# Outputs copied out two batch rows at a time, a re-ordered prologue and qd of chunk 1 on GpSimd, in a decay-attention and softplus-FFN kernel

## The chip, the cores and the metric

The kernel runs on one core of a Trainium2 chip. The metric is the device time of one execution in microseconds (us). Each kernel is run several times; the profile comes from one further execution on the same chip, whose own time is given beside its span (first to last instruction).

## What is computed

Decaying linear attention over 4 batch rows, 8 heads, 768 positions and head size 64, in blocks of 64 positions with a state carried from block to block, and then a feed-forward layer with softplus, 512 to 2048 to 512. All data are float32.

```python
rel = pos[:, None] - pos[None, :]
Dmask = np.where(rel >= 0, lam[:, None, None] ** rel[None, :, :], 0.0)
lam_pow = lam[:, None, None] ** (pos[None, :, None] + 1)
for b in range(nb):                                   # 12 blocks of 64
    intra = einsum('bhic,bhjc->bhij', qb, kb) * Dmask[None]
    intra = einsum('bhij,bhjd->bhid', intra, vb)
    inter = einsum('bhid,bhde->bhie', qb * lam_pow[None], kv_state)
    out[:, :, sl] = intra + inter
    kv_state = lam_block * kv_state + einsum('bhsd,bhse->bhde', kb * rev_pow, vb)
x = out.transpose(0, 2, 1, 3).reshape(B * S, H * D)
h = x @ w_in
y = (np.maximum(h, 0) + np.log1p(np.exp(-np.abs(h)))) @ w_out
```

## The kernel before

**Tiling.** The 768 positions are six chunks of 128 (two blocks of 64). A *unit* g is one chunk and one pair of heads: units 0 to 3 are chunk 0, units 4 to 7 chunk 1, 24 in all. A chunk's feed-forward layer has 16 *steps*, one per 128 hidden features; step number s runs over all chunks, 96 in all. The two large products keep float32 accuracy by splitting each operand into a high part (rounded to the float32r type) and a low part (the remainder): three matmuls take the place of one.

**A unit** has these parts. `k_decay` makes kd, k times the decay to the block's end (L259, two ScalarE instructions in every chunk). `q_decay` makes qd, q times the decay from the block's start (L265, two multiplications, on GpSimd in chunk 0 and on VectorE later). `mm_scores` (L273) multiplies k by q and kd by v into a two-bank PSUM tile. `mask_scores` (L303, VectorE) masks the scores; `first_states` (L317, ScalarE) or `second_states` and `update_states` (VectorE, L311) carry the state. `mm_out` (L287) makes the attention output; `x_high` (L333, ScalarE) and `x_low` (L340, VectorE) split it for the next product. For chunk 0 the tiles of kd, qd and masked scores are each unit's own; later they come from four rotating buffers (tag b2).

**A step** has `mlp1` (L359), 12 matmuls over the four pairs of heads; `chain_act` and `chain_lo` (L349, L355: softplus and copy on ScalarE, subtraction on VectorE); and, three steps later, `mlp2` (L373), 12 matmuls, three for each batch row, which accumulate over a chunk's 16 steps in two PSUM tiles `o` of two banks each. Tile 0 holds batch rows 0 and 1, tile 1 rows 2 and 3; the next chunk's tiles use the same banks. In a chunk's last `mlp2` each row's matmuls are followed at once by the row's copy out of PSUM, on ScalarE for even rows and on VectorE for odd ones, and by its transfer to memory on SP's queue. The last chunk cuts each row in two halves, one for each of the two engines, each with its own transfer on ScalarE's or SP's queue; its last `mlp2` takes two steps at once, six matmuls a row.

**The weights** arrive as packed blocks k = 0 to 31 in the order in which the steps use them, and are turned into high and low parts once: `w_scale` (two ScalarE instructions, L203 and L205), `w_bits` (three on VectorE, L209, L210, L213), `w_hi` (L216, a copy, on ScalarE unless VectorE is given) and `w_lo` (L220, VectorE). Blocks 0, 1 and 2 are converted one by one in the prologue, the rest in groups of two by the first steps: step s finishes one group and begins the next.

**What sets the order.** Nothing is reordered: each engine executes its instructions in the order in which the program lists them, and waits where data or buffers are not ready. The prologue is written out by hand (L420 to L464), with `begin(p)` (scores), `middle(p)` (state and mask) and `end(p)` (output) for the four units of chunk 0, the conversion of blocks 0 to 2 in between, and `keep_warm(n)`: n matmuls on zeros. The loop after it (L471) runs each step's parts in a fixed order. Scores of unit s//4 + 4 come at s % 4 = 1, its output at s % 4 = 3, and the kd of the next unit at s % 4 = 0. Loads are issued on SP, in an order of their own.

Of the kernel before, what the change touches and what calls it, by code (L numbers as in the profile page):

```python
# [7 lines left out]
F32 = mybir.dt.float32  # L8
# [6 lines left out]
B, H, S, D = 4, 8, 768, 64  # L15
C = 128
T = 64
NCH = S // C
NP = H // 2
NG = NCH * NP  # L20
# [11 lines left out]
def decay_attention_softplus_ffn(  # L32
# [7 lines left out]
    nc = tc.nc  # L40
# [7 lines left out]
    def t8(shape, dt, name):  # L48
        return sb.tile(shape, dt, tag="b8", bufs=21, name=name)
# [41 lines left out]
    def q_of(g):  # L91
        return part(g, 0, 0)
# [4 lines left out]
    def kt_of(g):  # L97
        return part(g, 1, 0)
# [46 lines left out]
    def keep_warm(n):  # L145
        for _ in range(n):
            nc.tensor.matmul(warm_ps, lhsT=warm[:, :128], rhs=warm, start=True, stop=True)  # L147

    keep_warm(30)

# [47 lines left out]
    def w_scale(ks):  # L200

        c = conv[ks[0]] = t4([128, len(ks), DM], U32, f"c{ks[0]}")
        nc.scalar.activation(c.bitcast(F32), raw_at(ks, 1).bitcast(F32), AF.Copy, scale=2.0**-112)  # L203

        nc.scalar.activation(raw_at(ks, 0), raw_at(ks, 0), AF.Copy, scale=2.0**-29)  # L205

    def w_bits(ks):
        c = conv[ks[0]]
        nc.vector.tensor_single_scalar(out=c, in_=c, scalar=3, op=ALU.logical_shift_left)  # L209
        nc.vector.scalar_tensor_tensor(  # L210
            out=c, in0=raw_at(ks, 1), scalar=0x80000000, in1=c, op0=ALU.bitwise_and, op1=ALU.bitwise_or
        )
        nc.vector.tensor_add(out=c, in0=c, in1=raw_at(ks, 0))  # L213

    def w_hi(ks, copy=nc.scalar.copy):
        copy(out=w_at(ks)[:, 0], in_=conv[ks[0]].bitcast(F32))  # L216

    def w_lo(ks):
        w = w_at(ks)
        nc.vector.tensor_sub(out=w[:, 1], in0=conv.pop(ks[0]).bitcast(F32), in1=w[:, 0])  # L220
# [19 lines left out]
    def heads(g):  # L240
        p = g % NP
        return slice(2 * p, 2 * p + 2)

    def first_chunk(g):
        return g < NP
# [6 lines left out]
    def own(g, n, name):  # L252
        if not first_chunk(g):
            return t2([128, B, 2, 64], F32, f"{name}_{g}")
        if g not in spares:
            spares[g] = t8([128, 3, B, 2, 64], F32, f"own_{g}")
        return spares[g][:, n]

    def k_decay(g):  # L259
        kd = kds[g] = own(g, 0, "kd")  # L260
        for t in range(2):
            h = heads(g).start + t
            nc.scalar.activation(kd[:, :, t], kt_of(g)[:, :, t], AF.Copy, scale=rp1[:, h : h + 1])  # L263

    def q_decay(g, eng):  # L265
        qd = qds[g] = own(g, 1, "qd")
        r = hi if first_chunk(g) else slice(0, 128)
        for t in range(2):
            w = lp[r, heads(g).start + t : heads(g).start + t + 1, :].broadcast_to([r.stop - r.start, B, T])
            eng.tensor_mul(out=qd[r, :, t], in0=q_of(g)[r, :, t], in1=w)  # L270


    def mm_scores(g, w):  # L273
# [59 lines left out]
    def x_high(g, w):  # L333

        nc.scalar.copy(  # L335
            out=x_of(g // NP, g % NP)[:, 0].rearrange("q (b s i) -> q s b i", b=B, s=2),
            in_=w[:, :, 0:256].rearrange("q s (b i) -> q s b i", b=B),
        )

    def x_low(g, w):  # L340
        x = x_of(g // NP, g % NP).rearrange("q n (b s i) -> q n s b i", b=B, s=2)
        nc.vector.tensor_sub(  # L342
            out=x[:, 1], in0=w[:, :, 0:256].rearrange("q s (b i) -> q s b i", b=B), in1=x[:, 0]
        )
# [14 lines left out]
    def mlp1(s, ps_=range(NP)):  # L359
        c, f = divmod(s, NF)  # L360
        if s not in h_tiles:
            h_tiles[s] = bank(f"h{s}")
        w = w_of(f, 0)
        for p in ps_:
            cs = slice(p * 128, (p + 1) * 128)
            x = x_of(c, p)
            for n, (i, j) in enumerate(((0, 0), (1, 0), (0, 1))):
                nc.tensor.matmul(  # L368
                    h_tiles[s], lhsT=w[:, i, cs], rhs=x[:, j, :],
                    start=p == 0 and n == 0, stop=p == NP - 1 and n == 2,  # L370
                )

    def mlp2(ss):  # L373
        c = ss[0] // NF
        ends = ss[-1] % NF == NF - 1
        if ss[0] % NF == 0:
            o_tiles[c] = [pair(f"o{c}_{bp}") for bp in range(2)]
        if ends:
            parts = [t8([128, B, 512], F32, f"ob{c}_{n}") for n in range(2 if c == NCH - 1 else 1)]
        for b in range(B):  # L380
            for s in ss:
                f = s % NF
                g, w = g_tiles[s], w_of(f, 1)
                for n, (i, j) in enumerate(((0, 0), (0, 1), (1, 0))):
                    nc.tensor.matmul(  # L385
                        o_tiles[c][b // 2][:, b % 2], lhsT=g[:, i, b * 128 : (b + 1) * 128], rhs=w[:, j],
                        start=f == 0 and n == 0, stop=f == NF - 1 and n == 2,
                    )
            if not ends:
                continue  # L390
            src = o_tiles[c][b // 2][:, b % 2]
            rows = slice(b * S + c * C, b * S + (c + 1) * C)
            if c == NCH - 1:
                nc.scalar.copy(out=parts[0][:, b, 0:256], in_=src[:, 0:256])
                nc.scalar.dma_start(out=out[rows, 0:256], in_=parts[0][:, b, 0:256])
                nc.vector.tensor_copy(out=parts[1][:, b, 0:256], in_=src[:, 256:512])
                nc.sync.dma_start(out=out[rows, 256:512], in_=parts[1][:, b, 0:256])
            else:
                if b % 2:
                    nc.vector.tensor_copy(out=parts[0][:, b], in_=src)  # L400
                else:
                    nc.scalar.copy(out=parts[0][:, b], in_=src)  # L402
                nc.sync.dma_start(out=out[rows, :], in_=parts[0][:, b])


    w0, z = {}, {}
# [1 line left out]
    def begin(p):  # L408
        w0[p] = pair(f"xy{p}")
        mm_scores(p, w0[p])  # L410

    def middle(p):
        first_states(p, w0[p])
        mask_scores(p, w0[p])

    def end(p):
        z[p] = work(f"z{p}")
        mm_out(p, z[p])

    for p in range(NP):  # L420
        q_decay(p, nc.gpsimd)
    k_decay(0)
    begin(0)
    keep_warm(2)
# [1 line left out]
    k_decay(1)  # L426
    end(0)
    x_high(0, z[0])
    x_low(0, z[0])
    begin(1)  # L430
    keep_warm(3)
    middle(1)
    end(1)
    x_high(1, z[1])
    x_low(1, z[1])
    k_decay(2)
    keep_warm(5)
    begin(2)
    keep_warm(5)
    w_scale([0])  # L440
    middle(2)
    k_decay(3)
    w_bits([0])
    end(2)
    x_high(2, z[2])
    x_low(2, z[2])
    begin(3)
    keep_warm(3)
    middle(3)
    w_hi([0], nc.vector.tensor_copy)  # L450
    w_lo([0])
    w_scale([1])
    end(3)
    mlp1(0, range(NP - 1))
    x_high(3, z[3])
    x_low(3, z[3])
    mlp1(0, range(NP - 1, NP))
    w_bits([1])
    w_hi([1], nc.vector.tensor_copy)
    w_lo([1])  # L460
    w_scale([2])
    k_decay(NP)
    w_bits([2])
    w_hi([2])  # L464

# [5 lines left out]
    for s in range(last + LAG):  # L471

        scores, outs = None, None
        if s % 4 == 1 and s // 4 + NP < NG:
            scores = s // 4 + NP
        if s % 4 == 3 and s // 4 + NP < NG:
            outs = s // 4 + NP
        if 0 <= s - 1 < last:
            chain_act(s - 1)
            chain_lo(s - 1)  # L480
        old, new = (w_group(s + 1) if s else [2]), w_group(s + 2)
        if s and old:
            w_hi(old)
        if new:
            w_scale(new)
        if old:
            w_lo(old)
        if new:
            w_bits(new)
        if s == last + LAG - 2:  # L490
            mlp2([s - LAG, s - LAG + 1])
        elif 0 <= s - LAG < last - 1:
            mlp2([s - LAG])
        if scores is not None:
            w = work(f"w{scores}")
            mm_scores(scores, w)
            mask_scores(scores, w)
            if scores < 2 * NP:
                second_states(scores - NP)
            update_states(scores, w)  # L500
            q_decay(scores, nc.vector)
        if s % 4 == 0 and s and s // 4 + NP < NG:
            k_decay(s // 4 + NP)
        if outs is not None:
            w = work(f"z{outs}")
            mm_out(outs, w)
            x_high(outs, w)
            x_low(outs, w)
        if 0 < s < last:
            mlp1(s)  # L510
        w_load(2 * s + (9 if s < 9 else 7))
        if s % 4 == 3:
            load_upto(s // 4 + NP + 2)
# [40 lines left out]
```

## Time and profile before

| | |
|---|---|
| median of 3 runs | 642.11 us (640.03, 642.11 and one of 2590.12) |
| the profiled execution | 640.66 us, span 638.9 us, mean granted TensorE clock 0.992 |
| PE busy | 609.5 us, 95% of the span, 5296 matmuls |
| VectorE (DVE) busy | 231.2 us, 36% |
| ScalarE (ACT) busy | 209.6 us, 33% |
| GpSimd (POOL) busy | 7.0 us, 1% |
| bytes moved | 48.99 MB, mean 77 GB/s |

The page gives shares of the whole span. The 40 slices below them are read next, since they tell stages apart: each slice is a fortieth of the span, and each digit the busy tenths of an engine in it. The chain of work that ended last goes back from the last instruction to what released it, and so on; a row is start, duration, engine, what it writes and the line. In the views of groups, idle time of an engine is listed with what ended it. "issue" is time in which the profile shows nothing that an engine waits for. Each float32 matmul of the attention appears as two instructions; a matmul's end is modelled.

### The profile page before, as it was taken

The numbers are of one execution on the slowest core, as the hardware profiler recorded it, in microseconds if no ns is written. First come the engines' busy times: TensorE is split into PE (matmuls) and PEld (weight loads), VectorE is DVE, ScalarE is ACT, GpSimd is POOL, SyncE is SP. The second block draws the span as 40 slices with busy tenths as digits, with TensorE's granted clock in tenths as the row PEclk, the third lists the DMA queues.
The fourth block names the chain that finished last, engine by engine and source line by source line (L and its number), as shares of the span: only waits on it lengthen the run. The fifth ranks groups of instructions, "written<-read, shape, count | busy, mean of one in ns | idle before, by whom it ended". The sixth has DMA issues, their size and how long they took to land.

```text
span 638.9 us, 11805 instructions
## 1 busy us (share of the span) xinstructions
PE 609.5 (95%) x5296; PEld 491.4 (77%) x5296; DVE 231.2 (36%) x360; ACT 209.6 (33%) x335; POOL 7.0 (1%) x16
## 2 busy tenths in 40 slices
PE   8787999998999998999998999999899999899996
PEld 6566778786888886888886888888688888688884
DVE  4389999953313313133133133132221221111111
ACT  2466776832222222322313222222323222222221
POOL 3000000000000000000000000000000000000000
PEclk9888999999999999999999999999999999999999
DMA  8993112323200221300111500102500100100001
GB/s 302 407 379 133 67 68 92 140 67 112 88 1 2 68 67 66 133 1 1 67 37 47 183 1 2 67 1 67 178 21 1 43 25 2 66 1 0 2 1 66
DMA packets 15747, 48.99 MB, mean 77 GB/s; under 512 B 1873, under 2 KB 2897, under 8 KB 15697
## 3 DMA queue, kind: packets, MB, share of 16 engines
q1 hardware_dynamic: 15120, 47.72, 20.8%
q8 instruction: 41, 0.67, 0.4%
q10 hardware_dynamic: 576, 0.52, 0.3%
q14 instruction: 10, 0.07, 0.0%
HBM read 41.95 MB, written 6.29 MB: 76 GB/s over the span
## 4 chain that ended last, share of the span: by engine, by line
PE 82%; DVE 10%; ACT 5%; issue 2%; DVEq 0%; ACTq 0%
PE h L368 37%; PE o L385 36%; DVE c L213 3%; PE w L280 2%; DVE c L210 2%; PE warm_ps L147 2%; PE z L294 2%; PE z L298 2%; DVE st L311 1%; DVE c L209 1%; DVE w L220 1%; ACT ob L402 1%; DVE g L357 1%; ACT c L203 1%; ACT l L351 1%
## 5 line engine op out<-in xcount | busy, mean ns | idle before, releaser
L385 PE MATMUL o<-w,g 128*128 128x512 f32 x1152 | 280.2, 390 | 11.7 <-ACT ob L402 9.1
L368 PE MATMUL h<-x,w 128*128 128x512 f32 x1152 | 285.1, 397 | 0.9 <-ACT l L351 0.9
L385 PEld LDWEIGHTS o<-w,g 128*128 128x128 f32 x1152 | 215.2, 188 | 61.4 <-ACT ob L402 13.3
L368 PEld LDWEIGHTS h<-x,w 128*128 128x128 f32 x1152 | 214.6, 189 | 47.9 <-ACT l L351 1.4
L357 DVE TENSOR_TENSOR g<-l,g 128x512 fp32r<-128x512 f32 x96 | 66.3, 691 | 285.5 <-ACT g L353 285.5
L351 ACT ACTIVATE l<-h 128x512 f32<-128x512 f32 x96 | 57.3, 597 | 306.4 <-PE h L368 298.2
L353 ACT CAST g<-l 128x512 fp32r<-128x512 f32 x96 | 59.6, 621 | 3.1
L342 DVE TENSOR_TENSOR x<-z,x 128x512 fp32r<-128x512 f32 x24 | 16.6, 690 | 48.5 <-ACT x L335 48.5
L311 DVE SCALAR_TENSOR_TENSOR st<-st,lam_c,w 64x256 f32<-64x256 f32 x72 | 31.7, 480 | 0.9
L335 ACT CAST x<-z 128x512 fp32r<-128x512 f32 x24 | 14.0, 584 | 50.7 <-PE z L298 50.7
L280 PEld LDWEIGHTS w<-att 64*64 64x64 f32 x640 | 21.2, 135 | 7.3 <-issue 5.6
L294 PEld LDWEIGHTS z<-qd,st 64*64 64x64 f32 x640 | 17.5, 136 | 11.6 <-issue 11.5
L282 PE MATMUL w<-att,kd 64*64 64x64 f32 x576 | 23.8, 222 | 2.6 <-ACT kd L263 2.4
L294 PE MATMUL z<-qd,st 64*64 64x64 f32 x640 | 21.5, 226 | 4.4 <-DVE qd L270 4.4
L280 PE MATMUL w<-att 64*64 64x64 f32 x640 | 24.7, 222 | 0.0
L306 DVE TENSOR_TENSOR a<-w,mask 128x512 f32<-128x512 f32 x20 | 13.8, 691 | 29.8 <-PE w L282 22.4
L216 ACT CAST w<-c 128x1024 fp32r<-128x1024 f32 (+1 forms) x16 | 16.0, 998 | 25.6 <-DVE c L213 25.6
L282 PEld LDWEIGHTS w<-att,kd 64*64 64x64 f32 x576 | 20.6, 135 | 3.4 <-ACT kd L263 3.4
L263 ACT ACTIVATE kd<-att,rp 128x256 f32<-128x256 f32 x40 | 18.1, 501 | 12.5 <-DMA att<-in_att 12.5
L220 DVE TENSOR_TENSOR w<-c,w 128x1024 fp32r<-128x1024 f32 (+1 forms) x18 | 19.9, 1106 | 4.6 <-ACT w L216 4.4
L213 DVE CUSTOM_DVE_ANT_0 c<-raw,c 128x2048 uint16<-128x2048 uint16 (+1 forms) x18 | 19.9, 1108 | 2.7 <-DVE c L210 0.6
L298 PE MATMUL z<-a,att 64*64 64x64 f32 x640 | 20.5, 221 | 0.0
(42 smaller groups left out, 205.2 us busy)
## 6 DMA issues: line engine op xcount, KB each, us to landing
att<-in_att SPq DMA_DIRECT2D x48, 512.0 KB, 4.7
raw<-in_wts SPq DMA_DIRECT2D x32, 512.0 KB, 10.2
out_dram<-ob SPq DMA_DIRECT2D x20, 256.0 KB, 2.3
out_dram<-ob ACTq DMA_DIRECT2D x4, 128.0 KB, 1.7
out_dram<-ob SPq DMA_DIRECT2D x4, 128.0 KB, 1.7
lam_b<-in_lam SPq DMA_DIRECT2D x1, 4.0 KB, 2.8
```

The costliest lines, as they stand in the source:

```text
L213: nc.vector.tensor_add(out=c, in0=c, in1=raw_at(ks, 0))
L220: nc.vector.tensor_sub(out=w[:, 1], in0=conv.pop(ks[0]).bitcast(F32), in1=w[:, 0])
L280: nc.tensor.matmul(w[r, 0, cols], lhsT=k[r, b, t], rhs=q[r, b, t], start=True, stop=True)
L282: nc.tensor.matmul(w[half(1 - s), 1, cols], lhsT=kd[r, b, t], rhs=v[r, b, t], start=True, stop=True)
L294: nc.tensor.matmul(w[half(t), s, cols], lhsT=st[r, b, t], rhs=qd[r, b, t], start=True, stop=False)
L298: nc.tensor.matmul(w[half(t), s, cols], lhsT=v[r, b, t], rhs=a[r, b, t], start=s == 0 and first_chunk(g), stop=True,)
L311: nc.vector.scalar_tensor_tensor(out=to[:, :, t], in0=of[:, :, t], scalar=lam_c[r, h : h + 1], in1=u[:, :, t], op0=ALU.mult, op1=ALU.add,)
L351: nc.scalar.activation(l_tiles[s], h_tiles.pop(s), AF.Softplus)
L353: nc.scalar.copy(out=g_tiles[s][:, 0, :], in_=l_tiles[s])
L357: nc.vector.tensor_sub(out=g[:, 1, :], in0=l_tiles.pop(s), in1=g[:, 0, :])
L368: nc.tensor.matmul(h_tiles[s], lhsT=w[:, i, cs], rhs=x[:, j, :], start=p == 0 and n == 0, stop=p == NP - 1 and n == 2,)
L385: nc.tensor.matmul(o_tiles[c][b // 2][:, b % 2], lhsT=g[:, i, b * 128 : (b + 1) * 128], rhs=w[:, j], start=f == 0 and n == 0, stop=f == NF ...
```

## The change

It has five parts.

1. *Outputs.* In a chunk's last `mlp2`, copies and transfers come after every second batch row: the even row's copy on ScalarE and the odd row's on VectorE, each of a whole row of 512. In the last chunk the rows are no longer cut in halves; ScalarE's queue issues the even rows' transfers and SP's the odd ones'.
2. *kd of chunk 0* is one VectorE multiplication by a broadcast operand, in place of two ScalarE instructions.
3. *qd* is one instruction a unit in place of two. Units 0 to 7 have it on GpSimd, before only units 0 to 3; from unit 8 on it stays on VectorE. It is issued with kd, at s % 4 = 0 in place of s % 4 = 1.
4. *The order of the prologue.* The conversion of block 0 lies between units 0 to 2 and that of block 1 around units 2 and 3; the copies `w_hi` of blocks 0 and 1 are ScalarE's; the parts of `mlp1(0)` run as soon as their units are done; 18 of 48 warm-up matmuls go.
5. *kd of unit 4* moves from the end of the prologue into step 0, behind the scaling of blocks 3 and 4.

```diff
-    keep_warm(30)
+    keep_warm(26)
...
     def k_decay(g):
         kd = kds[g] = own(g, 0, "kd")
+        if first_chunk(g):
+            w = rp1[:, heads(g)].rearrange("q (o t w) -> q o t w", o=1, w=1).broadcast_to([128, B, 2, D])
+            nc.vector.tensor_mul(out=kd, in0=kt_of(g), in1=w)
+            return
...
-    def q_decay(g, eng):
+    def q_decay(g):
         qd = qds[g] = own(g, 1, "qd")
         r = hi if first_chunk(g) else slice(0, 128)
-        for t in range(2):
-            w = lp[r, heads(g).start + t : heads(g).start + t + 1, :].broadcast_to([r.stop - r.start, B, T])
-            eng.tensor_mul(out=qd[r, :, t], in0=q_of(g)[r, :, t], in1=w)
+        eng = nc.gpsimd if g < 2 * NP else nc.vector
+        w = lp[r, heads(g), :].rearrange("q (o t) i -> q o (t i)", o=1).broadcast_to([r.stop - r.start, B, 2 * T])
+        eng.tensor_mul(
+            out=qd[r].rearrange("q b t i -> q b (t i)"), in0=q_of(g)[r].rearrange("q b t i -> q b (t i)"), in1=w
+        )
...
         if ends:
-            parts = [t8([128, B, 512], F32, f"ob{c}_{n}") for n in range(2 if c == NCH - 1 else 1)]
+            ob = t8([128, B, 512], F32, f"ob{c}")
...
-            if not ends:
+            if not ends or b % 2 == 0:
                 continue
-            src = o_tiles[c][b // 2][:, b % 2]
-            rows = slice(b * S + c * C, b * S + (c + 1) * C)
-            if c == NCH - 1:
-                nc.scalar.copy(out=parts[0][:, b, 0:256], in_=src[:, 0:256])
-                nc.scalar.dma_start(out=out[rows, 0:256], in_=parts[0][:, b, 0:256])
-                nc.vector.tensor_copy(out=parts[1][:, b, 0:256], in_=src[:, 256:512])
-                nc.sync.dma_start(out=out[rows, 256:512], in_=parts[1][:, b, 0:256])
-            else:
...
+            for n, copy in ((b - 1, nc.scalar.copy), (b, nc.vector.tensor_copy)):
+                copy(out=ob[:, n], in_=o_tiles[c][n // 2][:, n % 2])
+                queue = nc.scalar if c == NCH - 1 and n % 2 == 0 else nc.sync
+                queue.dma_start(out=out[n * S + c * C : n * S + (c + 1) * C, :], in_=ob[:, n])
...
     x_high(0, z[0])
+    begin(1)
+    keep_warm(2)
     x_low(0, z[0])
-    begin(1)
-    keep_warm(3)
     middle(1)
+    w_scale([0])
     end(1)
+    w_bits([0])
+    k_decay(2)
     x_high(1, z[1])
     x_low(1, z[1])
-    k_decay(2)
-    keep_warm(5)
+    w_hi([0])
     begin(2)
-    keep_warm(5)
-    w_scale([0])
     middle(2)
+    w_lo([0])
     k_decay(3)
-    w_bits([0])
     end(2)
+    mlp1(0, range(2))
     x_high(2, z[2])
+    begin(3)
     x_low(2, z[2])
-    begin(3)
-    keep_warm(3)
     middle(3)
-    w_hi([0], nc.vector.tensor_copy)
-    w_lo([0])
     w_scale([1])
+    w_bits([1])
+    mlp1(0, range(2, 3))
     end(3)
-    mlp1(0, range(NP - 1))
     x_high(3, z[3])
     x_low(3, z[3])
-    mlp1(0, range(NP - 1, NP))
-    w_bits([1])
-    w_hi([1], nc.vector.tensor_copy)
+    mlp1(0, range(3, 4))
+    w_hi([1])
+    w_scale([2])
     w_lo([1])
-    w_scale([2])
-    k_decay(NP)
     w_bits([2])
     w_hi([2])
...
             update_states(scores, w)
-            q_decay(scores, nc.vector)
-        if s % 4 == 0 and s and s // 4 + NP < NG:
+        if s % 4 == 0 and s // 4 + NP < NG:
             k_decay(s // 4 + NP)
+            q_decay(s // 4 + NP)
```

More of the change, by code (lines that the diff above doesn't have):

```diff
@@ L388, in mlp2 @@
                     )
-            if not ends:
+            if not ends or b % 2 == 0:
                 continue
-            src = o_tiles[c][b // 2][:, b % 2]
-            rows = slice(b * S + c * C, b * S + (c + 1) * C)
-            if c == NCH - 1:
-                nc.scalar.copy(out=parts[0][:, b, 0:256], in_=src[:, 0:256])
-                nc.scalar.dma_start(out=out[rows, 0:256], in_=parts[0][:, b, 0:256])
-                nc.vector.tensor_copy(out=parts[1][:, b, 0:256], in_=src[:, 256:512])
-                nc.sync.dma_start(out=out[rows, 256:512], in_=parts[1][:, b, 0:256])
-            else:
[L399 to L403, printed above, removed]
+            for n, copy in ((b - 1, nc.scalar.copy), (b, nc.vector.tensor_copy)):
+                copy(out=ob[:, n], in_=o_tiles[c][n // 2][:, n % 2])
+                queue = nc.scalar if c == NCH - 1 and n % 2 == 0 else nc.sync
+                queue.dma_start(out=out[n * S + c * C : n * S + (c + 1) * C, :], in_=ob[:, n])
     w0, z = {}, {}
@@ L420, in decay_attention_softplus_ffn @@
     for p in range(NP):
-        q_decay(p, nc.gpsimd)
+        q_decay(p)
     k_decay(0)
```

## The prediction

> **What bounds the kernel now.** I read the page's slices first, then the chain of work that ended last, then the groups and the timelines of single stages.
>
> ```profile
> PE   8787999998999998999998999999899999899996
> DVE  4389999953313313133133133132221221111111
> PEclk9888999999999999999999999999999999999999
> L385 PE MATMUL o<-w,g 128*128 128x512 f32 x1152 | 280.2, 390 | 11.7 <-ACT ob L402 9.1
> ```
>
> A slice is 16 us. There are three stages. Up to about 37 us is the prologue, with a clock below full. From there to about 119 us the DVE digits stand at 9: the conversion of the weights on VectorE sets the pace. After that only PE is full. Its one visible wait there is in the last row: the second MLP product waits for ACT's copy of an output, 9.1 us in all.
>
> That wait costs more than its row says. First the chain over two ordinary double steps and one in which a chunk of outputs ends, then that end:
>
> ```profile
> 132.25 2.95 PE h L368 x12
> ...
> 144.45 2.96 PE h L368 x12
> ...
> 159.05 2.95 PE h L368 x12
> ...
> 171.25 2.95 PE h L368 x12
> ```
> ```profile
> 148.68 0.49 ACT ob L402
> ...
> 149.22 1.67 PE o L385 x6
> ...
> 150.91 0.59 ACT ob L402
> ...
> 151.55 0.96 PE o L385 x3
> ```
>
> From 132.25 to 144.45 and from 159.05 to 171.25 the same pair of steps takes 12.20 us; from 144.45 to 159.05 it takes 14.60. The difference, 2.40, is the price of one chunk end. PE wants to write batch row 1 into the other half of the two-bank PSUM tile from which ACT copies row 0, and waits until that copy is over; the same happens between rows 2 and 3. Part of the 2.40 is the matmul pipeline, which runs empty each time.
>
> **The outputs in pairs.** Row 1's matmuls now come before row 0's copy, and row 3's before row 2's. The tile that PE writes next is the other pair, so nothing reads it. Five chunk ends times 2.40 is 12.0 us. What hides the copies then is the following first MLP product, 12 matmuls or 2.72 us at 0.227 each (worked out below), against copies that need these times:
>
> ```profile
> L400 DVE COPY ob<-o 128x512 f32<-128x512 f32 x10 | 6.9, 692 | 12.6 <-PE o L385 12.6
> L402 ACT COPY ob<-o 128x512 f32<-128x512 f32 x10 | 5.8, 582 | 8.7 <-PE o L385 8.7
> DVE own L306 <- ACT st L319: 8.4, 4, 5.0
> ```
>
> The third row (the view of waits) matters for their order: there too ACT and DVE read the two halves of one PSUM tile, and DVE begins only when ACT is done. So a pair takes 0.58 + 0.69 and two gaps of 0.03, about 1.33 us, one after the other. The last pair is free 1.33 us after its matmuls; PE asks for it no sooner than after 12 matmuls of the other product. Without that cover each chunk end would cost 1.33. Behind the copies on ACT stands the next softplus, which waits for that product anyway.
>
> The last chunk has no cover, and its copies were halves before:
>
> ```profile
> 624.64 4.09 PE o L385 x18
> ...
> 629.64 3.03 PE o L385 x12
> ...
> 633.58 1.67 PE o L385 x6
> ...
> 635.27 0.38 ACT ob L394
> ...
> 635.67 0.42 DVE ob L396
> ```
> ```profile
> out_dram<-ob SPq DMA_DIRECT2D x20, 256.0 KB, 2.3
> out_dram<-ob SPq DMA_DIRECT2D x4, 128.0 KB, 1.7
> ```
>
> The 18 matmuls that end at 628.73 take 0.227 us each. The other 18 would end at 628.73 + 4.08 = 632.81 without the two waits, instead of 635.24: 2.43 gained. Against it: the last two copies take 1.33 instead of 0.85 (635.24 to 636.09), 0.48 lost, and the last transfer is 256 KB, 2.3 us to landing instead of 1.7, 0.6 lost. Net 1.4 us. Bounds: 0.8 (ACT's copy behind a late transfer issue) to 2.0 (copies side by side).
>
> The Trainium skill ("PSUM — Partial Sum Buffer", section on bank collisions) says that two engines on different banks do not disturb each other; the two halves are different banks. By that rule the copies could run side by side, and the end would come some 0.6 us sooner; the wait row above speaks for the order that I take, since it is the program that makes DVE wait.
>
> **The prologue.** Its end is what the DVE stage starts from.
>
> ```profile
> 1.45 8.64 PE warm_ps L147 x30
> ...
> 16.35 1.68 issue
> ...
> 19.35 2.43 PE warm_ps L147 x5
> 22.92 1.36 PE warm_ps L147 x5
> 28.45 1.96 issue
> ```
> ```profile
> 16.35:28.45 12.10, 10.15 (x254) 7.79 (x254) 5.17 (x9) 6.21 (x12) 0.68 (x1) 0.86 1.03 407
> ```
> ```profile
> 42.30 1.05 ACT L216 CAST w<-c 128x1024 fp32r<-128x1024 f32 x1 [1.21 <-DVE c L213]
> ```
> ```profile
> 7.95 0.91 ACT L263 ACTIVATE own<-att,rp 128x256 f32<-128x256 f32 x2 [5.94 <-DMA att<-in_att]
> 31.66 0.69 DVE L342 TENSOR_TENSOR x<-z,x 128x512 fp32r<-128x512 f32 x1 [2.89 <-ACT x L335]
> 32.27 0.42 DVE L209 TENSOR_SCALAR c<-c 128x512 uint32<-128x512 uint32 x1
> 34.64 0.69 DVE L220 TENSOR_TENSOR w<-c,w 128x512 fp32r<-128x512 f32 x1
> 36.53 0.69 DVE L213 CUSTOM_DVE_ANT_0 c<-raw,c 128x1024 uint16<-128x1024 uint16 x1
> ```
>
> *Order of the conversion.* From x_low of unit 3 at 31.66, VectorE is never idle: conversion of weight block 1 (32.27 to 34.64, with the copy of its high part), its low part at 34.64, block 2 until 37.22. In the change the bits of block 1 are made before that x_low, in the 2.89 us in which VectorE waits for it, and the high part is ACT's. So the work between 32.27 and 34.64 leaves this place: 2.4 us. ACT's copy (about 0.6, as the row of L402 for that size) runs beside x_low (0.69). If the cover were too short (the bits are 1.9 of the 2.4 us), the excess would come back; bounds 1.5 to 2.4.
>
> *PE's part.* Four warm-up matmuls fewer at the start is 4 x 0.227 = 0.9 us sooner, and kd of unit 0 is there: one multiplication of 0.69 us, started at 7.95, ends before the 26 are through. The 0.69 for a kd on VectorE is the row of the equally large x_low, against 0.91 for ACT's two; three of the four stand where VectorE waits, and the fourth, kd of unit 3, lies ahead of x_low of unit 2, behind PE's own work. The warm-ups after unit 1 (2.43) leave the chain. Those at 22.92 hid the state copy and the mask (0.58 and 0.69, by the rows of that size), which stay. Six matmuls of the first MLP product come in before unit 3, at 0.23 to 0.43 us each (1.4 to 2.6). And two stalls named "issue" stay: PE stops at 16.35 and again 254 matmuls and 254 weight loads later, with the DMA engines full (share 1.03). I read this as the fetch of instructions (the page has a DMA queue of that name) behind the loads. It comes at a fixed count of instructions, and 36 fewer do not carry either stall out of the prologue; a stall met earlier may simply last longer. So x_high of unit 3 comes between 0 and 2.6 us sooner than at 31.05; I take 1.5.
>
> Prologue together: 2.4 + 1.5 = 3.9 us (bounds 1.5 and 5.0). kd of unit 4, moved behind the scaling of blocks 3 and 4 on ACT, costs 0.9 us of ACT ahead of the first softplus, and ACT idles 1.21 us before its copy at 42.30: nothing, or 0.9 if that cover is gone. No DMA is issued in another place on SP; the loads run ahead of their use by more than the shift.
>
> **qd on GpSimd.** The DVE stage ends where PE waits for kd of unit 7, at 118.97:
>
> ```profile
> 51.29 0.76 DVE L270 TENSOR_TENSOR qd<-att,lp 128x256 f32<-128x256 f32 x2
> ```
> ```profile
> 118.17 0.80 ACT kd L263 x2
> ```
> ```profile
> 13.06 1.42 POOL L270 TENSOR_TENSOR own<-att,lp 64x256 f32<-64x256 f32 x2 [2.42 <-DMA att<-in_att]
> 14.32 0.69 DVE L342 TENSOR_TENSOR x<-z,x 128x512 fp32r<-128x512 f32 x1 [1.76 <-ACT x L335]
> ```
>
> Units 4, 5 and 6 have their qd before that point, 0.76 us each with VectorE busy without a break around it; 3 x 0.76 = 2.3 us. GpSimd does as many elements per partition in 1.42, and it is issued a step before the scores and read three steps after. Unit 7's lies behind the point and gains nothing, nor does merging two instructions into one from chunk 2 on: VectorE is at a third there. What GpSimd's work costs VectorE beside it no row shows directly. Nearest is the pair above: VectorE's 14.32 instruction overlaps GpSimd's and still takes 0.69. So zero; the other bound is the whole GpSimd instruction, 3 x 1.42 = 4.3 us, a net loss of 2.0.
>
> **Sum**, against the profiled execution's 640.66 (span 638.9; the median of the three runs is 1.45 higher): 640.66 - 12.0 - 1.4 - 3.9 - 2.3 = 621.1 us.
>
> **Rivals.**
> *GpSimd holds VectorE.* In the stage at 9s nearly every VectorE instruction reads two operands from SBUF; the row at 14.32 reads one from PSUM, so it excludes little. If GpSimd's instruction blocks them for its length, three of them cost 4.3 and save 2.3: 640.66 - 17.3 + 2.0 = 625.4. The Trainium skill ("SBUF — State Buffer", "Who interferes with whom") states just this: a VectorE instruction with two SBUF inputs contends with a GpSimd one that reads SBUF, and the later one waits for all of it. No row here tests that rule.
> *The prologue gives nothing.* Fewer warm-ups, a slower clock (already 0.86 between the stalls), and stalls that end when the fetch ends: 640.66 - 15.7 = 625.0. For it speaks that the second stall's end at 30.41 may hang on the loads alone; against it, that 2.4 of the 3.9 do not depend on PE.
> *The wait at the chunk end only moves*, to the next chunk's first rows: half of 12.0 remains, about 627.1. Against it: 2.7 us of cover for 1.33.
> *Slower: each copy waits for the transfer of the row before it*, since all four fill one tile. Then the four copies take 2 x 1.27 + 3 x 2.3 = 9.4 us from 148.7 on, to 158.1, and PE, 30 matmuls after 147.41 (the rest of this product, the other one, the first pair), wants the second pair at 154.2: 3.9 lost per chunk end, 19.5 in all, and 6.9 in the last. 640.66 - 12.0 + 19.5 + 6.9 - 1.4 - 6.2 = 647.5. It decides from a stall of 2.4 per chunk end on. Against it:
>
> ```profile
> 149.19 4.48 SPq L403 DMA_DIRECT2D out_dram<-ob  x4
> 150.29 0.69 DVE L400 COPY ob<-o 128x512 f32<-128x512 f32 x1 [0.88 <-PE o L385]
> ```
>
> The copy of row 1 began 1.1 us after row 0's transfer was issued, before its 2.3 were over, in the same tile.
>
> **Chances.** Forecast 0.48, GpSimd's hold 0.27, no gain in the prologue 0.15, the moved wait 0.08, slower 0.02. The range goes from 617.0 (prologue 5.0, tail 2.0, and some waits of VectorE for ACT gone too) to 627.0, which takes in three rivals' centres but not two of them together. 2% is 12.8 us, about what a measurement of this kernel tells from no change: 627.9 is the line. The chunk ends alone nearly reach it, and any one other term carries it over; faster 0.88, within 10 in 100, slower 2 in 100.
>
> **What would show it.** In the profile after: pairs of steps across a chunk end at 12.2 us; no wait of PE for an output copy; the last copies on ACT and DVE in turn; x_high of unit 3 near 29.5 and block 2's bits finished near 33.3 instead of 37.22; VectorE instructions of unchanged length with no gaps while GpSimd works (gaps of over 1 us would be the hold); PE free of the DVE stage near 112.8. A chunk end above 12.2, a stall in the prologue that outlasts 31 us, or an idle VectorE beside GpSimd each prove one term wrong.

## The result, and the profile after

| | before | after |
|---|---|---|
| median of the runs | 641.55 us (4 runs, one of them 2590.12) | 625.56 us (4 runs, 625.08 to 625.74) |
| profiled execution, span | 640.66, 638.9 us | 625.08, 623.3 us |
| VectorE, ScalarE, GpSimd busy | 231.2, 209.6, 7.0 us | 230.2, 208.2, 12.7 us |

The ratio, which leaves out the run of 2590.12 us, is 0.9757, with a 95% interval of 0.9737 to 0.9778: about 16 us faster. The forecast was 621.1 (617 to 627), so the direction and the range held, and the gain fell short by 4 us. The measured 625.1 is also what two of the rivals had named (GpSimd's hold 625.4, no gain in the prologue 625.0), so the time alone cannot tell them apart. The rows can.

The end of a chunk first: rows of the chain that ended last (start, duration, engine, what it writes, line), over the same stretch of steps as before.

```profile
118.28 2.99 PE h L374 x12
...
130.52 2.95 PE h L374 x12
...
142.72 2.95 PE h L374 x12
...
154.92 2.95 PE h L374 x12
...
167.12 2.95 PE h L374 x12
```
```profile
L391 PE MATMUL o<-w,g 128*128 128x512 f32 x1152 | 276.4, 389 | 0.0
```

Every pair of steps now takes 12.20 us, the one with the chunk end (142.72 to 154.92) too; it was 14.60. The group of the second product (from the page) has no idle time left in front of it, where it had 11.7 us. The last chunk runs through as well:

```profile
610.88 8.17 PE o L391 x36
...
619.07 0.59 ACT ob L398
...
619.69 0.69 DVE ob L398
```

36 matmuls without a break, then the last pair's copies in turn, ScalarE before VectorE, as forecast. From the last copy's end to the end of the span it is 2.92 us, against 2.81 before: the larger transfer cost 0.1, not 0.6.

Now the prologue and the conversion stage. First x_high of unit 3, with which the prologue ends, before the change, then the same in the changed kernel (ScalarE's timelines) with VectorE's rows from there on:

```profile
31.05 0.58 ACT L335 CAST x<-z 128x512 fp32r<-128x512 f32 x1 [2.93 <-PE z L298]
```

```profile
32.03 0.59 ACT L341 CAST x<-z 128x512 fp32r<-128x512 f32 x1 [0.71 <-PE z L304]
```
```profile
32.08 0.69 DVE L213 CUSTOM_DVE_ANT_0 c<-raw,c 128x1024 uint16<-128x1024 uint16 x1
32.69 0.68 DVE L348 TENSOR_TENSOR x<-z,x 128x512 fp32r<-128x512 f32 x1
33.46 0.69 DVE L220 TENSOR_TENSOR w<-c,w 128x512 fp32r<-128x512 f32 x1
...
35.35 0.69 DVE L213 CUSTOM_DVE_ANT_0 c<-raw,c 128x1024 uint16<-128x1024 uint16 x1
```

Block 1's bits do lie before x_low of unit 3 (32.69), and block 2 is done at 36.04, 4.01 us after x_high began; before, it took 6.17 us. But x_high itself came 1 us later, not 1.5 sooner. And VectorE instructions beside GpSimd's are longer. GpSimd's rows for units 5, 6 and 7 (unit 4's qd lies in the prologue, at 24.81), and VectorE's beside them:

```profile
41.52 1.30 POOL L274 TENSOR_TENSOR qd<-att,lp 128x512 f32<-128x512 f32 x1 [15.45 <-PE w L288]
...
66.56 1.51 POOL L274 TENSOR_TENSOR qd<-att,lp 128x512 f32<-128x512 f32 x1 [23.73 <-ACT g L359]
...
110.27 1.82 POOL L274 TENSOR_TENSOR qd<-att,lp 128x512 f32<-128x512 f32 x1 [42.20 <-DMA att<-in_att]
```
```profile
42.19 1.72 DVE L220 TENSOR_TENSOR w<-c,w 128x1024 fp32r<-128x1024 f32 x1 [0.51 <-ACT w L216]
...
66.83 1.78 DVE L363 TENSOR_TENSOR g<-l,g 128x512 fp32r<-128x512 f32 x1
...
111.08 2.10 DVE L213 CUSTOM_DVE_ANT_0 c<-raw,c 128x2048 uint16<-128x2048 uint16 x1
```

These three take 1.22, 0.69 and 1.23 us elsewhere. Each ends about its usual length after GpSimd's instruction has ended: 41.52 + 1.30 = 42.82, and 42.19 + 1.72 = 43.91 is 1.09 later.

### The profile page after: what moved, and what is told of

Same layout as the page of the kernel before. It is cut to its first block, busy times and chain, and to the rows that moved or that the text cites. A ratio compares the mean times of both kernels' runs of the same rounds, so it can differ in the third digit from the quotient of the medians.

```text
span 623.3 us, 11732 instructions
## 1 busy us (share of the span) xinstructions
PE 604.4 (97%) x5278; PEld 492.1 (79%) x5278; DVE 230.2 (37%) x336; ACT 208.2 (33%) x327; POOL 12.7 (2%) x16
## 4 chain that ended last, share of the span: by engine, by line
PE 84%; DVE 11%; issue 2%; ACT 2%; DVEq 0%; ACTq 0%
PE h L374 38%; PE o L391 37%; DVE c L210 2%; PE w L286 2%; DVE c L213 2%; PE z L300 2%; PE z L304 2%; DVE w L220 1%; PE warm_ps L147 1%; DVE c L209 1%; DVE st L317 1%; DVE g L363 1%; ACT w L216 1%; PE w L288 1%; PE xy L286 0%
## 5 line engine op out<-in xcount | busy, mean ns | idle before, releaser
L391 PE MATMUL o<-w,g 128*128 128x512 f32 x1152 | 276.4, 389 | 0.0
L286 PE MATMUL w<-att 64*64 64x64 f32 x640 | 26.0, 226 | 0.0
L216 ACT CAST w<-c 128x1024 fp32r<-128x1024 f32 (+1 forms) x18 | 17.2, 956 | 22.4 <-DVE c L213 22.4
L220 DVE TENSOR_TENSOR w<-c,w 128x1024 fp32r<-128x1024 f32 (+1 forms) x18 | 20.4, 1132 | 4.0 <-ACT w L216 3.8
L213 DVE CUSTOM_DVE_ANT_0 c<-raw,c 128x2048 uint16<-128x2048 uint16 (+1 forms) x18 | 20.8, 1156 | 2.5
L210 DVE SCALAR_TENSOR_TENSOR c<-raw,c 128x1024 uint32<-128x1024 uint32 (+1 forms) x18 | 19.9, 1107 | 0.6
```

Source lines behind the costliest of these rows:

```text
L210: nc.vector.scalar_tensor_tensor(out=c, in0=raw_at(ks, 1), scalar=0x80000000, in1=c, op0=ALU.bitwise_and, op1=ALU.bitwise_or)
L286: nc.tensor.matmul(w[r, 0, cols], lhsT=k[r, b, t], rhs=q[r, b, t], start=True, stop=True)
L391: nc.tensor.matmul(o_tiles[c][b // 2][:, b % 2], lhsT=g[:, i, b * 128 : (b + 1) * 128], rhs=w[:, j], start=f == 0 and n == 0, stop=f == NF ...
```

## The experiments

Three times, all read from each run's profile, separate what the runs mix: W, the end of the first warm-up matmuls in the chain; X, the start of x_high of unit 3; and F, the first step of the steady stage (the row at 120.05 before and at 118.28 after). X - W is the rest of the prologue, F - X the conversion stage.

| run | W | X | X - W | F - X | ratio to before (95%) |
|---|---|---|---|---|---|
| before | 10.09 | 31.05 | 20.96 | 89.00 | |
| after | 10.46 | 32.03 | 21.57 | 86.25 | 0.9757 (0.9737 to 0.9778) |
| e1_pairs_only | 11.35 | 32.80 | 21.45 | 88.98 | 0.9798 (0.9781 to 0.9815) |
| e2_rest_only | 10.06 | 32.48 | 22.42 | 86.24 | 0.9974 (0.9964 to 0.9984) |
| e3_qd_vector | 8.97 | 31.34 | 22.37 | 84.39 | 0.9719 (0.9706 to 0.9733) |
| e4_qd_twice | 9.49 | 32.11 | 22.62 | 88.43 | 0.9802 (0.9787 to 0.9817) |
| e5_writes_only | 9.69 | 32.46 | 22.77 | 87.53 | 0.9788 (0.9771 to 0.9804) |
| e6_six_tiny | 10.04 | 31.04 | 21.00 | 86.25 | 0.9748 (0.9729 to 0.9767) |
| e7_unit3_first | 10.35 | 32.57 | 22.22 | 86.03 | 0.9750 (0.9735 to 0.9764) |
| e8_qd_in_shadow | 9.07 | 31.38 | 22.31 | 84.44 | 0.9726 (0.9711 to 0.9740) |
| f1_qd_vector_old_place | 9.32 | 31.75 | 22.43 | 86.18 | 0.9757 (0.9738 to 0.9776) |
| f2_vector_tiny | 10.37 | 33.53 | 23.16 | 84.38 | 0.9732 (0.9715 to 0.9749) |
| f3_vector_tiny_mlp_late | 9.21 | 30.90 | 21.69 | 84.20 | 0.9706 (0.9692 to 0.9720) |
| f4_vector_mlp_late | 10.39 | 32.47 | 22.08 | 84.20 | 0.9712 (0.9696 to 0.9728) |

F - X repeats to 0.02 us where the code of that stage is the same (89.00 and 88.98; 86.25, 86.24 and 86.25; 84.39 and 84.38). In e7, which differs from the changed kernel only ahead of X, it is 0.22 less. So differences of 0.2 us are not read as anything, and those of 1 us or more are. W and X - W cannot: W differs by up to 1.5 us between executions of the same warm-up, and X by 1.75 between the two runs that share the prologue of before.

### One part at a time

**e1_pairs_only**: the kernel before, with the output code of the change.

```diff
...
-            if not ends:
+            if not ends or b % 2 == 0:
                 continue
...
+            for n, copy in ((b - 1, nc.scalar.copy), (b, nc.vector.tensor_copy)):
+                copy(out=ob[:, n], in_=o_tiles[c][n // 2][:, n % 2])
...
```

> The kernel before with the output copies in pairs, and nothing else changed. Theory A (the chain of the changed kernel): five chunk ends of 2.40 us and 2.43 us in the last chunk are gained, 0.6 us of the tail is given back, 13.8 us in all: span near 625.1 us, pairs of steps across a chunk end at 12.20 us, and the prologue as before (x_high of unit 3 near 31 us, first steady step near 120 us). Rival B (the prologue and qd bring a good part of the gain, and paired outputs less): span above 629 us.

**e2_rest_only**: the changed kernel, with the output code of before (the same diff backwards).

> The changed kernel with the old output copies: only the new prologue and qd on GpSimd. Theory A: first steady step near 118.3 us instead of 120.05, chunk ends at 14.6 us again, span near 637.1 us, so less than 0.4% gained. Rival B (the prologue and qd bring the 6.2 us of the forecast where the output copies do not get in their way): span near 632.7 us.

Measured: 0.9798 for the pairs alone, about 13 us, and 0.9974 for all the rest, under 2 us. Chain rows of the pairs alone and of the rest alone:

```profile
133.99 2.95 PE h L368 x12
...
146.19 2.95 PE h L368 x12
...
158.38 2.95 PE h L368 x12
```
```profile
130.94 2.95 PE h L374 x12
...
143.13 2.96 PE h L374 x12
...
157.74 2.95 PE h L374 x12
```

Pairs alone give 12.20 and 12.19 us; the rest alone keeps the 14.61 us of the chunk end. From F to the start of ScalarE's last copy it is 500.76 (e1) and 500.79 us (changed kernel) with pairs, 515.23 (e2) and 515.22 (before) without: 14.4 to 14.5 us less, where five times 2.40 and 2.43 make 14.43. The span of e1 (626.8) missed the expected 625.1 by 1.7 us, and its X came 1.75 us later than in the kernel before. Theory A holds, rival B falls.

### What GpSimd's work costs

**e3_qd_vector**: qd of units 4 to 7 on VectorE, at the new place.

```diff
-        eng = nc.gpsimd if g < 2 * NP else nc.vector
+        eng = nc.gpsimd if g < NP else nc.vector
```

> The changed kernel with qd of units 4 to 7 on VectorE, as one instruction at the new place. Theory A (GpSimd holds VectorE, and takes back most of what it saves): VectorE instructions of 1.72, 1.78 and 2.10 us fall back to 1.22, 0.69 and 1.23, qd costs 0.7 us per unit instead, and the first steady step comes 0.3 to 1.0 us later than in the changed kernel; time within 0.2% of it. Rival B (no hold; the long instructions have another cause): they stay long, and the first steady step comes 2.1 us or more later.

Measured: the long instructions are gone, as theory A said, but F - X fell to 84.39, 1.86 us *less* than with GpSimd, where A expected the first steady step 0.3 to 1.0 us later and B 2.1 or more. Neither had seen what VectorE's timeline shows:

```profile
39.16 1.23 DVE L213 CUSTOM_DVE_ANT_0 c<-raw,c 128x2048 uint16<-128x2048 uint16 x1
40.31 0.68 DVE L274 TENSOR_TENSOR qd<-att,lp 128x512 f32<-128x512 f32 x1
40.91 0.69 DVE L363 TENSOR_TENSOR g<-l,g 128x512 fp32r<-128x512 f32 x1
41.51 1.22 DVE L220 TENSOR_TENSOR w<-c,w 128x1024 fp32r<-128x1024 f32 x1
```

In a step without scores VectorE has to wait 0.5 us for ScalarE's high part (the row at 42.19 above: 0.51, "ACT w L216"). qd, moved one step ahead, now lies in that gap, and the wait in front of L220 is gone. This new theory C was tested by moving it back.

**f1_qd_vector_old_place**: e3 with qd of units 4 to 7 behind the update of the states again.

```diff
             update_states(scores, w)
+            if scores < 2 * NP:
+                q_decay(scores)
...
-            q_decay(s // 4 + NP)
+            if s // 4 + NP >= 2 * NP:
+                q_decay(s // 4 + NP)
```

> The kernel e3_qd_vector with qd of units 4 to 7 back behind the update of the states (s % 4 = 1) on VectorE, still as one instruction. Theory C (what helps is the place: one step earlier qd fills the half microsecond in which VectorE waits for ACT's high-part copy, and GpSimd's work only costs): from x_high of unit 3 to the first steady step 1.5 to 2.1 us more than in e3_qd_vector (84.39), so 85.9 to 86.5, and the 0.5 us waits of VectorE for ACT are back. Rival D (the place does not matter, one instruction in place of two is the gain): 84.2 to 84.8 us, as in e3_qd_vector.

Measured: 86.18, inside C's interval, and the wait is back:

```profile
41.90 1.23 DVE L220 TENSOR_TENSOR w<-c,w 128x1024 fp32r<-128x1024 f32 x1 [0.51 <-ACT w L216]
49.81 0.69 DVE L274 TENSOR_TENSOR qd<-att,lp 128x512 f32<-128x512 f32 x1
```

So the place is worth 1.79 us, and GpSimd takes back 1.86. On GpSimd at the new place (86.25) qd costs as much as on VectorE at the old one (86.18).

**e4_qd_twice**: the multiplication of units 4 to 7 done twice.

```diff
-        eng.tensor_mul(
+        for _ in range(2 if NP <= g < 2 * NP else 1):
+            eng.tensor_mul(
...
```

> The changed kernel with the qd multiplication of units 4 to 7 done twice in a row on GpSimd (same operands, same result). Theory A (a GpSimd instruction that reads SBUF and a VectorE instruction with two SBUF operands exclude each other): three further VectorE instructions in the stage of the weights' conversion are lengthened, by up to 1.3 us each, and the first steady step comes 1.5 to 3.9 us later. Rival B (no exclusion): nothing moves, since GpSimd has whole steps to spare.

Measured: F - X 88.43, 2.18 more, within A's 1.5 to 3.9. One pair of GpSimd's and two VectorE instructions beside it:

```profile
41.61 3.54 POOL L275 TENSOR_TENSOR qd<-att,lp 128x512 f32<-128x512 f32 x2 [14.29 <-PE w L289]
```
```profile
42.27 1.72 DVE L220 TENSOR_TENSOR w<-c,w 128x1024 fp32r<-128x1024 f32 x1 [0.51 <-ACT w L216]
43.91 1.78 DVE L209 TENSOR_SCALAR c<-c 128x1024 uint32<-128x1024 uint32 x1
```

By their lengths they take turns: GpSimd, VectorE, GpSimd (whose two instructions now span 3.54 us), VectorE. In the whole stage six VectorE instructions are lengthened, three more than in the changed kernel. The second one held, L209, has only one SBUF operand and takes 0.69 elsewhere, so "two SBUF operands" was too narrow.

**e5_writes_only**: three fills of the qd tile on GpSimd first.

```diff
+        for _ in range(3 if NP <= g < 2 * NP else 0):
+            eng.memset(qd, 0.0)
         eng.tensor_mul(
```

> The changed kernel with three fills of the qd tile on GpSimd ahead of the multiplication for units 4 to 7, about 1.6 us of GpSimd work per unit that writes SBUF and reads none. Theory A (the exclusion is between reads): VectorE instructions with two SBUF operands keep their length beside the fills and only the multiplication lengthens one, so the first steady step stays within 0.7 us of the changed kernel's 118.28. Rival B (any GpSimd work holds VectorE): three more instructions are lengthened, and the step comes 1.5 us or more later.

Measured, in GpSimd's and VectorE's timelines:

```profile
41.96 1.69 POOL L275 MEMSET qd<- 128x512 f32 x3 [16.02 <-PE w L290]
43.73 1.29 POOL L276 TENSOR_TENSOR qd<-att,lp 128x512 f32<-128x512 f32 x1
```
```profile
42.62 1.23 DVE L220 TENSOR_TENSOR w<-c,w 128x1024 fp32r<-128x1024 f32 x1 [0.51 <-ACT w L216]
43.76 1.81 DVE L209 TENSOR_SCALAR c<-c 128x1024 uint32<-128x1024 uint32 x1
```

The fills hold nothing: L220, with two SBUF operands, keeps its 1.23 beside them. The multiplication behind them holds L209. By the time of F rival B was right and A wrong: 119.99, 1.7 us later than 118.28, where B asked for 1.5 and A allowed 0.7. By the rows it is the other way round. Three VectorE instructions are lengthened up to F, as many as in the changed kernel, each beside a multiplication and none beside a fill. Two of the three holds now cost about 0.6 us more each, since the fills push the multiplication away from the half microsecond in which VectorE waits for ScalarE; X was 0.4 us later. So A's mechanism stands, and its time was wrong for a reason that the rows show.

**e8_qd_in_shadow**: GpSimd's qd held back until the second states are made, so that it runs beside their update.

```diff
                 second_states(scores - NP)
+                nc.gpsimd.tensor_copy(out=lam_b[lo, 0:1], in_=states[scores][lo, 3, 1, 0:1])
+                q_decay(scores)
             update_states(scores, w)
...
-            q_decay(s // 4 + NP)
+            if s // 4 + NP >= 2 * NP:
+                q_decay(s // 4 + NP)
```

> The changed kernel with GpSimd's qd of units 4 to 7 started only when VectorE has made the second states, by a one-column copy of them that GpSimd does first, so that it runs beside the update of the states, whose second operand is in PSUM. Theory A (only VectorE instructions with two SBUF operands are held): no VectorE instruction is lengthened, the 0.76 us of qd stays saved in full, and the first steady step comes 1.0 to 2.0 us sooner than in the changed kernel, near 116.7. Rival B (every VectorE instruction is held): the updates are lengthened by 0.5 to 1.3 us per unit, and the step comes no sooner than 118.

```profile
47.88 1.29 POOL L274 TENSOR_TENSOR qd<-att,lp 128x512 f32<-128x512 f32 x1
```
```profile
47.63 1.79 DVE L317 SCALAR_TENSOR_TENSOR st<-st,lam_c,w 64x256 f32<-64x256 f32 x4
```

The four updates, one operand in SBUF and one in PSUM, keep their 1.79 us, and F - X is 84.44, 1.8 us less than in the changed kernel: theory A. (F itself, 115.82, came 2.5 us sooner, more than A's 1.0 to 2.0, since X was 0.65 sooner as well.) GpSimd's work costs VectorE nothing here, and is worth as much as the better place on VectorE.

The Trainium skill ("SBUF — State Buffer", "Who interferes with whom") fits all four: a VectorE instruction with two SBUF inputs and a GpSimd one that reads SBUF exclude each other, a GpSimd one that only writes does not take part, and a VectorE `tensor_scalar` can use both ports in its fast mode and is then held as well. L209 agrees: 1024 elements in 0.69 us, against 1.23 for L210's.

### What ends the prologue

**e6_six_tiny**: six warm-up matmuls of 32 columns behind the 26.

```diff
     keep_warm(26)
+    for _ in range(6):
+        nc.tensor.matmul(warm_ps[:, :32], lhsT=warm[:, :128], rhs=warm[:, :32], start=True, stop=True)
```

> The changed kernel with six warm-up matmuls of 32 columns (a tenth of a microsecond in all or little more) behind the 26: 12 more PE instructions. Theory A (PE stops at fixed counts of instructions, and a block of instructions is asked for when the one before it begins; with 8 instructions fewer that point has slipped behind the wait for the first state): the packets of the instruction queue come at 15.3, 21.8 and 27.8 us again instead of 16.3, 22.8 and 28.8, the first stall ends about 1 us sooner, and x_high of unit 3 comes about 1 us sooner than at 32.03. Rival B (the clock alone makes the prologue late): the stall ends as late as before, x_high within 0.4 us of 32.03.

Measured: X at 31.04, and packets of the instruction queue at 14.6, 20.7 and 26.9 us: the interval that theory A named, and each 0.7 to 1.1 us sooner than it had them. But W differs between executions, so one run is thin evidence. The same six were added to e3.

**f2_vector_tiny**: e3 with the six tiny matmuls (the same diff).

> The kernel e3_qd_vector with the six tiny matmuls behind the first warm-up. Theory A (the fetch of the next block of PE instructions is asked for earlier): the first packet of the instruction queue within 4.8 us of the end of the 26 warm-ups (5.4 in e3_qd_vector), the first stall shorter by 0.8 us or more, x_high of unit 3 sooner by 0.3 to 1 us reckoned from the end of the warm-ups, time 0 to 0.15% lower than e3_qd_vector. Rival B (no effect beyond the spread of the warm-up phase): the same within 0.2 us.

Measured: first packet at 16.4, 6.0 us after W, and X - W 23.16, 0.8 *more* than e3, about as much as the lengthened instruction below adds. Theory A fails; the six are worth nothing that these runs can tell. What f2 does show is the hold in the prologue itself, between GpSimd's qd of unit 2 (13.13 to 14.39 in its timeline) and VectorE's new kd of unit 1 (chain):

```profile
12.72 0.69 DVE own L314
13.41 1.55 DVE own L265
```

0.69 became 1.55, on the path; before, kd of chunk 0 was ScalarE's. In six more runs with the changed prologue (e2, e4, e5, e6, f1 and f3) the path holds a lengthened instruction at this place too, 0.8 to 1.0 us longer than elsewhere, but one of block 0's conversion, which the new order put there. In the other five, the changed kernel among them, the path has none: in the changed kernel kd takes 0.68 and GpSimd's multiplication 1.57.

**e7_unit3_first**: the first six matmuls of the MLP product behind unit 3's scores.

```diff
-    mlp1(0, range(2))
     x_high(2, z[2])
     begin(3)
+    mlp1(0, range(2))
```

> The changed kernel with the scores of unit 3 ahead of the first six matmuls of the MLP product instead of behind them. Theory A (these six, at half clock 2.65 us, stand in front of unit 3 on PE): scores, state and mask of unit 3 come 2.6 us sooner, and x_high of unit 3 between 1.0 and 2.6 us sooner, unless the next block of instructions is then late; time 0.2 to 0.4% lower. Rival B (the third fetch of instructions, with its packet at 28.75, sets the end whatever stands before it): a stall of 1 to 2 us appears in the output of unit 3, and x_high stays within 0.5 us of 32.03.

Measured: X at 32.57, nothing gained, 0.54 us from the 32.03 where rival B allowed 0.5, but without B's stall. Unit 3's state copy did come sooner, 17.2 us after W against 19.1. In the changed kernel six matmuls stand ahead of unit 3's scores; here nine stand ahead of its output (chains of the two):

```profile
25.77 2.65 PE h L374 x6
```
```profile
27.46 3.99 PE h L374 x9
```

0.44 us each, twice the 0.227 of the steady stage. The granted clock is low in this part of the prologue. These are the windows of the changed kernel and of the kernel before from 20 to 25 us (the clock is the third number from the end):

```profile
20.00:25.00 5.00, 3.41 (x94) 2.87 (x90) 2.58 (x4) 1.68 (x3) 0.19 (x1) 0.50 1.02 404
```
```profile
20.00:25.00 5.00, 5.00 (x112) 3.59 (x114) 2.04 (x4) 3.29 (x7) 0.00 (x0) 0.81 1.02 405
```

Where the clock falls differs between executions: e2, with the new prologue, has 0.87 from 20 to 25 us and 0.50 from 25 to 30; e1, with the one of before, has 0.66 and 1.00. Over the whole stretch from 10 to 31 us it is 0.92 in both runs with the prologue of before, and 0.68 to 0.84 in the twelve with the new one. That the missing warm-ups are the reason is a reading: no run put them back.

**f3_vector_tiny_mlp_late** and **f4_vector_mlp_late**: f2 and e3 with all twelve behind unit 3, as in the kernel before.

```diff
-    mlp1(0, range(2))
...
-    mlp1(0, range(2, 3))
...
-    mlp1(0, range(3, 4))
+    mlp1(0)
```

> The kernel f2_vector_tiny with all twelve matmuls of the first MLP product behind unit 3's output, as in the kernel before. Theory A (six to nine of them at half clock, 2.7 to 4.0 us, stand in front of unit 3 on PE): the state copy of unit 3 comes 2 us sooner or more and x_high of unit 3 1 to 2.5 us sooner; the twelve run in the shadow of the conversion; time 0.15 to 0.4% lower than f2_vector_tiny. Rival B (the third block of instructions, whose packet comes at about 27 us, ends the prologue): a stall of 1.5 us or more in the output of unit 3, x_high within 0.5 us of f2_vector_tiny.

> The same as f3_vector_tiny_mlp_late without the six tiny matmuls. Theory A (the matmuls in front of unit 3 are what delays it): x_high of unit 3 1 to 2.5 us sooner than in e3_qd_vector, as in f3. Rival B (the fetch ends the prologue): x_high within 0.5 us of e3_qd_vector, and 0.5 us or more later than in f3, reckoned from the end of the warm-ups.

Measured: the state copy of unit 3 comes 17.7 us (f3) and 17.9 us (f4) after W, against 19.9 in e3, so the matmuls did stand in the way. Against f2, which its expectation names, f3's X - W is 1.5 us less and its time 0.27% lower, as theory A had it; but f2 has the hold on kd besides. Against e3, X - W falls by only 0.7 (f3) and 0.3 (f4), the latter within rival B's 0.5. Most of the 2 us is lost again in the output of unit 3: a stall of 0.55 or 0.66 us returns there, and from 25 to 35 us the granted clock is 0.50 in both, against 0.67 and 1.00 in e3. The truth lies between A and B. f3, with a median of 621.98 us (0.9706), is the fastest of these kernels, about 3.3 us below the changed one by the ratios, though its interval overlaps those of f4 and e3.

## Why the prediction was right, and where it fell short

| step | forecast | profiled pair |
|---|---|---|
| five chunk ends and the last chunk's waits | 12.0 + 2.43 | 14.4 |
| tail given back | -1.08 | -0.6 |
| prologue: order of the conversion | 2.4 | 2.2 |
| qd on GpSimd | 2.3 | 0.2 |
| one wait of VectorE | none | 0.4 |
| prologue: PE's part | 1.5 | -1.0 (X) |
| sum | 19.5 | 15.6 (638.9 - 623.3) |

The 2.2, 0.2 and 0.4 are parts of one measured number, the 2.75 us by which F - X fell; how it divides is said below.

*The outputs in pairs: right to a few hundredths.* The price of 2.40 per chunk end was read from the period of the steps, not from the wait's own row, which says 9.1 us in all. The serial copies of a pair, 1.33 us, were right, and are hidden as said. Only the transfer of 256 KB was priced too high.

*The order of the conversion: right in size.* From x_high to the end of block 2's bits it is 4.01 us instead of 6.17: 2.2 of the 2.4. In f1, where qd is on VectorE at its old place, F - X is 2.8 below the kernel before. Beside the 2.2, VectorE's timelines show 0.2 for one qd instruction in place of two and 0.4 for a wait of 0.56 us in front of one L213 (at 56.21 before), which is there in e1 too and in no run with the new prologue; the forecast did not have it, and why it went is open.

*qd on GpSimd: this step failed.* The forecast took "zero" for what GpSimd costs VectorE, from a row in which VectorE's second operand came from PSUM, and gave the hold a chance of 0.27. The hold is real: it takes back 1.86 us of what the better place brings (84.39 against 86.25). The price that the rival gave it, 4.3 us, was the whole of GpSimd's work; the measured one is less, since part of each hold fell on time in which VectorE waited anyway, or on an instruction that was under way. The 2.3 was a little high as well: a pair of qd instructions takes 0.76 us to its end, but the next one starts 0.68 after it (51.29 to 51.97), so three make 2.0. Taking this work off VectorE is worth 1.74 us where GpSimd holds nothing (e8 against f1), and the better place on VectorE is worth the same 1.79 (e3 against f1). The changed kernel has neither: it is level with f1.

*PE's part of the prologue: this step failed too.* The start did come sooner: W is 9.68 on average over the eight runs whose warm-up and prologue are those of the change (10.46, 10.06, 8.97, 9.49, 9.69, 10.35, 9.07 and 9.32, one of them with another place for six matmuls), and 10.72 over the two of before, near the 0.9 forecast, though two runs are few. But the stretch behind it grew by as much: X - W is 22.3 on average against 21.2, so X, on average 32.0 against 31.9, did not move. The runs show three things in that stretch that the sum had not priced, or had priced too low: a granted clock of 0.68 to 0.84 in place of 0.92, six matmuls at 0.44 us ahead of unit 3, and, in seven of the twelve runs, a VectorE instruction on the path beside GpSimd's qd that is 0.8 to 1.0 us longer than elsewhere. How much each takes, and what the two stalls depend on, stays open: X moves by more than a microsecond between executions of the same prologue, and shifting the count of instructions did not move the stalls in the way that the reading as instruction fetch asks.

That X came 1.0 later in the profiled pair, and not 0.1 as on average, is such a spread. The rival "the prologue gives nothing" was half right: PE's part gave nothing, the order gave 2.2 of its 2.4. GpSimd's hold came true in kind, at 1.86 us for the 4.3 that it was given. The other rivals fell: no chunk end above 12.2, and no copy behind a transfer.

So the forecast was right in its direction for the reason that it gave, since the outputs alone bring 14 us. That the time fell within the range owes as much to the range, which took in both rivals that came half true.

## What to carry to other kernels

Price a recurring wait by the difference between two periods, one with it and one without; its own idle row missed a quarter of the cost here (9.1 of 12.0 us). The matmuls right behind the waits make up the rest: the groups of six and of three took 1.67 and 0.96 us, about 0.3 longer each than at 0.227 a matmul, which the prediction reads as the pipeline refilling. Before work is moved to GpSimd, look at what VectorE does at that moment: beside the instructions of the weights' conversion, most of which read two SBUF operands, it saved almost nothing here; beside the update of the states, which reads PSUM, it cost nothing. And look for a half microsecond of waiting on the same engine first; one step earlier, qd cost VectorE almost nothing.

## What the runs showed of the hardware that was not expected

- The same 26 warm-up matmuls from 1.45 us on took 7.52 to 9.01 us in different executions, and 30 took 8.64 and 9.90. When PE comes to its full pace is not fixed: counted in windows of 1.5 us, e3 has 8 of these matmuls from 4.5 us on, while the changed kernel has 4 or 5 until 7.5 us and 8 only then. The granted clock reads 1.00 in all these windows.
- GpSimd's multiplication of 128x512 took 1.27 to 1.30 us alone and up to 1.82 beside VectorE in the changed kernel, 2.14 in e5: it is held too.
- The granted clock of the prologue is lower with the new order (0.68 to 0.84 from 10 to 31 us, against 0.92), and the 5 us in which it is at half are not the same ones in every execution.
